# Linear attention and a low-rank mixer on one core: batch 0's q loaded, featured and transposed by halves of its heads

## The chip, the cores and the metric

The kernel runs on one core of one Trainium2 chip. The metric is the time of one execution on the device in microseconds, as the median of the timed runs; the profile is of one execution of its own.

## The reference

There are two parts, one behind the other, for 8 batches of 576 rows; attention has 8 heads of 64 columns, the mixer works on 512 columns.

```python
theta = pi / 2 * arange(S) / S
phi(x) = concat([relu(x) * cos(theta), relu(x) * sin(theta)])      # 64 -> 128 features
q_p, k_p = phi(q), phi(k)
kv  = einsum('bhsf,bhsd->bhfd', k_p, v)
z   = sum(k_p, axis=2)
x   = einsum('bhsf,bhfd->bhsd', q_p, kv) / (einsum('bhsf,bhf->bhs', q_p, z) + 1e-6)
x   = x with the heads side by side: (8, 576, 512)
u   = x + (x^T @ U @ V)^T                       # U: 576 x 32, V: 32 x 576
out = u + relu(u @ w_ch1) @ w_ch2               # 512 -> 2048 -> 512
```

Inputs and output are float32; the kernel multiplies in bf16.

## The kernel before

A batch's 576 rows are nine for each of 64 row groups, which are laid on 128 partitions: even partitions take five of the nine (chunks 0 to 3 and a tail, chunk 4), odd partitions take four. So a batch of q, k or v comes in two loads: `load_odd` (L80, 64 partitions x 8 heads x 256 columns, 512 KiB) and `load_even` (L74, 64 x 8 x 320, 640 KiB). Both take a range of heads; batch 0's v uses it and comes in four loads. SyncE issues them in program order: q, k and v of batch 0 first.

The schedule is written out by hand: each engine executes its instructions in the order of the program text, and an instruction that waits holds up what stands behind it on its engine. The program has a long list of slots from batch 0's first mixer matmuls on, in which TensorE is fed without a stop, and a part ahead of it, which the change touches. That part, for batch 0, goes like this:

- `keep_warm` issues matmuls of a zero tile (L202), four of 512 and 72 of 128 columns, while the first loads are on their way.
- `q_prep` (by `prep` and `scaled_relu`, L305 on ScalarE, L307 on VectorE) makes the features of one chunk of q: relu times the cosine weight on VectorE, relu times the sine weight on ScalarE, each 128 x 512. For chunk 3 VectorE makes both (`FEATS`). `qtr_mm` (L394) transposes a chunk's eight heads on TensorE into a bank `t_q[c]`, and one 512-wide filler follows each chunk.
- `qtr_evac` (by `cast`, L114 on ScalarE, L116 on VectorE) copies a bank into `q_pT` or, for the tail, `q_tlT`. Chunks 0 to 2 are copied ahead of k's features, chunk 3 and the tail behind them, both on ScalarE.
- `k_prep` makes k's features in the order 0, 1, 2, 4, 3, and `z_mm` (L1219) sums each chunk with 48 columns of ones, eight matmuls a chunk, into a tile `xz`. `spread_v` (L235) spreads the small matrix V over four quarters.
- `first_chain` casts v to bf16 (`v0`), copies z, and interleaves on TensorE: `kv0_mm` (L353) for heads 0 and 1, `den_mm` (L1227) for chunks 0 to 2, `kv0_mm` for heads 2 and 3, `den_mm` for chunks 3 and 4. Then come the reciprocal (L429, L430), the products of q^T with kv (L1235), their division (L1244), kv of heads 4 to 7 (`kv_unit`, L341), and the mixer's first steps, up to `g1_open` (L727), which starts the dense part.

Weights come on GpSimd's queue. `mark` copies hold them back: `w1_load(0)` goes out once a one-element copy has read the tail of q's features, `w1_load(1)` to `(3)` once one has read `q_tlT`, and `w2_all` (L1385, in slot 6) once batch 1's `q_pT` is there; then four loads of w2 follow, a quarter (four of sixteen row blocks) each. SyncE's queue is held in the same way: q of batch 1 waits for k's first feature, k and v of batch 1 for z.

The functions that the change touches:

Of the kernel before, what the change touches and what calls it, by code (L numbers as in the profile page):

```python
# [17 lines left out]
def kernel(  # L18
# [11 lines left out]
    nc = tc.nc  # L30

    B = 8
    H = 8
# [3 lines left out]
    P = 128  # L37
# [11 lines left out]
    def tail(b):  # L49
# [23 lines left out]
    def load_even(dst, src, b, h0=0, h1=H):  # L73
        nc.sync.dma_start(  # L74
            out=dst[0:P:2, h0:h1].rearrange("m h c d -> m h (c d)"),
            in_=nines(src, b)[:, h0:h1, 0 : 5 * D],
        )
# [25 lines left out]
            out=w1_bf[:, :, cs], in_=moe_w_ch1.rearrange("(d p) n -> p d n", p=P)[:, :, cs]  # L103
        )

    def w2_load(n):
        js = slice(n * 4, n * 4 + 4)
        nc.gpsimd.dma_start(
            out=w2_bf[:, js, :], in_=moe_w_ch2.rearrange("(j p) n -> p j n", p=P)[:, js, :]
        )  # L110

    def cast(eng, o, i):
        if eng is nc.scalar:
            nc.scalar.activation(out=o, in_=i, func=AF.Copy, bias=0.0, scale=1.0)  # L114
        else:
            eng.tensor_copy(out=o, in_=i)  # L116


    V_, A_, G_ = nc.vector, nc.scalar, nc.gpsimd
# [4 lines left out]
    zero = pool.tile([P, 512], BF16, tag="o_sb", bufs=2, name="zero")  # L124
# [1 line left out]
    for x in (qst, kst, vst):  # L126
        V_.memset(x[:, :, 4, :], 0.0)
    load_odd(qst, q, 0)
    load_even(qst, q, 0)
    load_odd(kst, k, 0)  # L130
    load_even(kst, k, 0)
    for h0 in (0, 4):
# [2 lines left out]
    v0 = pool.tile([P, H, 5, D], BF16, tag="hid", bufs=1, name="v0")  # L135

    def load_uv():
# [16 lines left out]
        out=iota[:, 0:4], pattern=[[2, 4]], base=0, channel_multiplier=9,  # L154
        allow_small_or_imprecise_dtypes=True,
    )
    for lo in (0, TS):
        nc.gpsimd.iota(
            out=iota[lo : lo + TS, 4:5], pattern=[[1, 1]], base=8, channel_multiplier=18,
# [3 lines left out]
        out=iota[:, 5:6], pattern=[[1, 1]], base=8, channel_multiplier=9,  # L163
# [21 lines left out]
    q_tl = const.tile([P, H, 2 * D], BF16)  # L185
    q_tlT = const.tile([P, H, P], BF16)
    x_tl = const.tile([P, DM], BF16)
    U_bf = const.tile([P, 6, R], BF16)
    V_bf = const.tile([P, 4, P], BF16)
# [9 lines left out]
    def keep_warm(n, tag, bufs, cols=512):  # L199
        w_ps = ps.tile([P, 512], FP32, tag=tag, bufs=bufs, name="w_ps")  # L200
        for _ in range(n):
            nc.tensor.matmul(  # L202
                out=w_ps[:, 0:cols], lhsT=zero[:, 0:P], rhs=zero[:, 0:cols], start=True, stop=True
            )
# [3 lines left out]
    mark = const.tile([TS, 1], FP32)  # L208
# [141 lines left out]
    def kv0_mm(b, acc, hs):  # L350
        for h in hs:
            for c in range(5):
                nc.tensor.matmul(  # L353
                    out=acc[:, h, :], lhsT=k_p[b][:, c, h, :] if c < 4 else k_tl[:, h, :],
                    rhs=v0[:, h, c, :], start=(c == 0), stop=(c == 4),
                )
# [35 lines left out]
    def qtr_mm(b, c, h0, h1, t):  # L392
        for h in range(h0, h1):
            nc.tensor.transpose(  # L394
                out=t[:, h, :], in_=q_p[b][:, c, h, :] if c < 4 else q_tl[:, h, :],
                identity=ident,
            )

    def qtr_evac(b, c, eng, t):
        if c < 4:  # L400
            cast(eng, q_pT[b][:, c, :, :], t)
        else:
            cast(eng, q_tlT[:, :, tail(b)], t[:, :, 0:P:2])
# [634 lines left out]
    ORD = (4, 0, 1, 2, 3)  # L1038
# [185 lines left out]
    def den_mm(b, d, cs):  # L1224
        for c in cs:
            for h in range(H):
                nc.tensor.matmul(  # L1227
                    out=d[:, c, h, :], lhsT=qT_of(b, c, h),
                    rhs=z_sb[:, h : h + 1].to_broadcast([P, 12]), start=True, stop=True,
                )  # L1230
# [39 lines left out]
                scale=rec[rows, c, h0 + i : h0 + i + 1],  # L1270
            )

    def first_chain(b, xz, z, v_ps):
        def fill(n):
            for _ in range(n):
                nc.tensor.matmul(
                    out=xz[:, 1, P:512], lhsT=zero[:, 0:P], rhs=zero[:, 0:384],
                    start=True, stop=True,
                )

        d = xz[:, 1, 0:480].rearrange("p (c h n) -> p c h n", h=H, n=12)
        rec = pool.tile([P, 5, H], FP32, tag="rec5", bufs=1, name="rec5")
        cast(V_, v0[:, 0:2], vst[:, 0:2])
        cast(V_, z_sb, z[:, :, 0])
        cast(V_, v0[:, 2:4], vst[:, 2:4])
        cast(V_, v0[:, 4:6], vst[:, 4:6])
        qtr_evac(b, 4, A_, t_q[4])
        kv_sb[b] = pool.tile([P, H, E], BF16, tag="kv", bufs=2, name="kv")
        acc = bank([P, 4, D], FP32, *G3, "kv_ps")
        kv0_mm(b, acc, (0, 1))  # L1290
        den_mm(b, d, (0, 1, 2))
        kv0_mm(b, acc, (2, 3))
        cast(A_, V_bf, v_ps.rearrange("r (c p) -> r c p", c=4))
        cast(A_, kv_sb[b][:, 0:4, 0:D], acc)
        cast(A_, v0[:, 6:H], vst[:, 6:H])
        den_mm(b, d, (3, 4))
        recip(rec, d[:, :, :, 0])
        x0 = [xh_mm(b, c, 0, *G3) for c in ORD[0:2]]
        kv_unit(b, 1, *T1, A_)
        x0 += [xh_mm(b, c, 0, *t) for c, t in zip(ORD[2:5], (G3, OA, OB))]  # L1300
        xh_norm_act(b, ORD[4], 0, rec, x0[4])
        for n in range(4):
            xh_norm(b, ORD[n], 0, rec, x0[n])
# [24 lines left out]
        open_mm(b, 3, uT_ps[b, 3], range(4))  # L1328
# [2 lines left out]
    qT_alloc(0)  # L1331
    cast_uv()
    keep_warm(4, "X", 1)
    keep_warm(72, "X", 1, P)
    t_q = []
    for c in TL:
        tg = G3 if c < 3 else O2()
        t_q.append(bank([P, H, P], BF16, *tg, "t_ps"))
    for c in TL:
        q_prep(0, c, FEATS[c])  # L1340
        qtr_mm(0, c, 0, H, t_q[c])
        keep_warm(1, "X", 1)
    for c, eng in zip(TL[0:3], (V_, A_, V_)):
        qtr_evac(0, c, eng, t_q[c])
    xz = ps.tile([P, 2, 512], FP32, tag="X", bufs=1, name="xz")
    z = xz[:, 0, 0:384].rearrange("p (h n) -> p h n", n=48)
    v_ps = None
    for n, c in enumerate(KORD):
        k_prep(0, c, (V_, A_ if c < 4 else V_))
        if n < 2:  # L1350
            keep_warm((1, 2)[n], *T1)
        if n == 2:
            v_ps = spread_v(*T1)
        z_mm(0, c, z)
    qtr_evac(0, 3, A_, t_q[3])

    G_.tensor_copy(out=mark[0:1], in_=q_tl[0:1, 0, 0:1])
    w1_load(0)
    nc.sync.dma_start(out=mark2, in_=k_p[0][0:1, 0, 0, 0:1])
    load_odd(qst, q, 1)  # L1360
    load_even(qst, q, 1)
    first_chain(0, xz, z, v_ps)
    G_.tensor_copy(out=mark[0:1], in_=q_tlT[0:1, 0, 0:1])
    for n in range(1, 4):
        w1_load(n)
    nc.sync.dma_start(out=mark2, in_=z_sb[0:1, 0:1])
# [16 lines left out]

    def w2_all():
        G_.tensor_copy(out=mark[0:1], in_=q_pT[1][0:1, 3, 0, 0:1])  # L1385
        for n in range(4):
            w2_load(n)

    at(6, w2_all)
# [109 lines left out]
```

## Time and profile before

| | |
|---|---|
| time, median of 3 runs | 291.11 us (290.12 to 291.51) |
| the profiled execution, its own time | 290.06 us |
| its span | 288.3 us |
| TensorE, matmuls | 282.3 us busy, 98% |
| TensorE, weight loads | 211.8 us, 73% |
| VectorE | 218.6 us, 76% |
| ScalarE | 179.7 us, 62% |
| GpSimd | 71.3 us, 25% |
| moved by DMA | 53.32 MB, 185 GB/s over the span |

The profile of one execution names engines PE (TensorE matmuls), PEld (its weight loads), DVE (VectorE), ACT (ScalarE), POOL (GpSimd) and SP (SyncE); a q behind the name (SPq) stands for the engine's issuing side. A row of the timeline gives the start in us from the span's start, the length in us from the first start to the last end of the merged instructions, engine, line and operation, tile written and tiles read, shapes, and how many were merged; brackets hold idle time ahead of it and what ended it. Instructions overlap by a little, so an engine's pace is read from start to start. A row of the groups has the count, then the busy sum in us and the mean in ns. A row of the windows has the stretch, its length, the busy time with the count of instructions that touch it, the granted clock, the share of the DMA engines and GB/s. A row of the chain gives start, length and what the end waited for.

### The profile page before, as it was taken

What the parts mean: (1) busy time and instruction counts of PE and PEld (TensorE: products, weight loads), DVE (VectorE), ACT (ScalarE), POOL (GpSimd) and SP (SyncE); (2) the same over time, 40 slices, a digit from 0 to 9 for tenths busy, and PEclk for the clock granted to TensorE, in tenths of its full rate; (3) what the DMA queues carried; (4) which work ended last, traced back from release to release, by engine and by line L of the source; (5) the groups of instructions that cost most, each with busy time, mean ns of one, the idle gap of its engine ahead of it and who ended that gap; (6) DMA issues with size and microseconds to landing.
All of it is one profiled execution on the core that took longest, in us unless ns stands there. A gap on an engine that the chain in (4) does not pass through costs nothing.

```text
span 288.3 us, 7567 instructions
## 1 busy us (share of the span) xinstructions
PE 282.3 (98%) x3097; PEld 211.8 (73%) x3122; DVE 218.6 (76%) x449; ACT 179.7 (62%) x316; POOL 71.3 (25%) x111
## 2 busy tenths in 40 slices
PE   8999999999999999999999999999999999999995
PEld 6886455545887756876887667876888778899884
DVE  4979738886887688569895388958894689689864
ACT  2965651576687576986587588876797772177110
POOL 8330600050035304641006500351005000400140
PEclk9999999999999999999999999999999999999999
DMA  6999999999969999799829993489939400610023
GB/s 202 336 282 253 292 207 264 275 184 200 285 174 169 241 354 202 193 268 282 230 41 188 303 279 106 84 146 200 312 40 177 164 1 10 154 77 2 0 90 131
DMA packets 85447, 53.32 MB, mean 185 GB/s; under 512 B 53990, under 2 KB 83078, under 8 KB 85414
## 3 DMA queue, kind: packets, MB, share of 16 engines
q1 hardware_dynamic: 78998, 41.62, 61.5%
q0 software_dynamic: 6272, 11.17, 16.5%
q8 instruction: 24, 0.39, 0.5%
q10 hardware_dynamic: 144, 0.07, 0.1%
q14 instruction: 9, 0.07, 0.1%
HBM read 36.86 MB, written 9.44 MB: 161 GB/s over the span
## 4 chain that ended last, share of the span: by engine, by line
PE 97%; DVE 1%; issue 1%; DVEq 0%
PE w_ps L892 30%; PE g_ps L710 22%; PE al_ps L653 8%; PE be_ps L653 6%; PE gt_ps L741 5%; PE o_ps L781 5%; PE w_ps L202 3%; PE x_ps L439 3%; PE kv_ps L364 3%; PE ot_ps L801 2%; PE ot_ps L994 2%; PE a_ps L465 1%; PE va_ps L495 1%; PE t_ps L382 1%; PE t_ps L394 1%
## 5 line engine op out<-in xcount | busy, mean ns | idle before, releaser
L710 PE MATMUL g_ps<-uT,w_bf 128*128 128x512 bf16 x281 | 71.5, 380 | 0.7
L717 ACT ACTIVATE hid<-g_ps 128x512 bf16<-128x512 f32 x76 | 45.0, 597 | 26.2 <-PE g_ps L710 24.0
L912 POOL TENSOR_TENSOR o_sb<-o_sb,u_bf 128x512 f32<-128x512 f32 x21 | 25.6, 1232 | 110.6 <-DVE o_sb L912 110.6
L892 PEld LDWEIGHTS <-hid 128*128 128x128 bf16 x448 | 43.1, 98 | 5.7 <-DVE hid L857 0.2
L710 PEld LDWEIGHTS <-w_bf 128*128 128x128 bf16 x298 | 27.5, 98 | 23.8
L678 DVE TENSOR_TENSOR hid<-pw,be_ps 128x512 bf16<-128x512 f32 x39 | 26.7, 686 | 16.6 <-PE be_ps L653 9.4
L892 PEld LDWEIGHTS <-S 128*128 128x128 bf16 x336 | 32.2, 98 | 4.5
L114 ACT ACTIVATE pw<-al_ps 128x512 f32<-128x512 f32 x39 | 23.1, 595 | 15.4 <-PE al_ps L653 9.7
L892 PE MATMUL w_ps<-T,hid 128*128 128x256 bf16 x224 | 27.9, 273 | 0.0
L892 PE MATMUL w_ps<-w_bf,hid 128*128 128x256 bf16 x224 | 27.6, 273 | 0.0
L892 PE MATMUL w_ps<-T,S 128*128 128x256 bf16 x224 | 27.1, 273 | 0.0
L114 ACT ACTIVATE o_sb<-w_ps 128x512 f32<-128x512 f32 x21 | 12.5, 597 | 20.5 <-PE w_ps L892 14.1
L912 DVE TENSOR_TENSOR o_sb<-o_sb,w_ps 128x512 f32<-128x512 f32 x21 | 14.4, 685 | 13.7 <-ACT o_sb L114 9.6
L653 PEld LDWEIGHTS <-sa 128*128 128x128 bf16 x208 | 19.3, 98 | 4.9 <-issue 0.3
L506 DVE TENSOR_TENSOR u_bf<-x_bf,va_ps 128x1024 bf16<-128x1024 bf16 (+1 forms) x20 | 19.5, 1000 | 3.0 <-PE va_ps L495 3.0
L449 DVE TENSOR_TENSOR x_bf<-x_ps,rec 128x512 bf16<-128x512 f32 x28 | 19.4, 692 | 1.0
L116 POOL CAST v_ext<-vst 128x512 bf16<-128x512 f32 x24 | 16.4, 722 | 7.8 <-DMA vst<-in_v_dram 4.5
L653 PEld LDWEIGHTS <-w_bf 128*128 128x128 bf16 x156 | 15.2, 98 | 4.0 <-issue 0.2
L305 ACT ACTIVATE k_p<-kst,sinw 128x512 bf16<-128x512 f32 x26 | 18.0, 713 | 0.0
L741 PE MATMUL gt_ps<-uT_tl,w_bf 128*128 128x128 bf16 x256 | 16.4, 219 | 0.0
L653 PE MATMUL al_ps<-tb,sa 128*128 128x256 bf16 x104 | 15.6, 273 | 0.2
L781 PE MATMUL o_ps<-w_bf,hid 128*128 128x512 bf16 x61 | 15.3, 380 | 0.2
(192 smaller groups left out, 509.1 us busy)
## 6 DMA issues: line engine op xcount, KB each, us to landing
qst<-in_q_dram SPq DMA_DIRECT2D x14, 512.0 KB, 5.9
kst<-in_k_dram SPq DMA_DIRECT2D x14, 512.0 KB, 8.6
vst<-in_v_dram SPq DMA_DIRECT2D x12, 512.0 KB, 8.7
out_dram<-o_sb POOLq DMA_DIRECT2D x12, 512.0 KB, 6.7
w_bf<-in_moe_w_ch_dram POOLq DMA_DIRECT2D x8, 512.0 KB, 10.4
out_dram<-o_sb SPq DMA_DIRECT2D x4, 512.0 KB, 3.0
qst<-in_q_dram SPq DMA_DIRECT2D x2, 640.0 KB, 5.7
kst<-in_k_dram SPq DMA_DIRECT2D x2, 640.0 KB, 13.8
```

The lines of the kernel that those rows point to most:

```text
L114: nc.scalar.activation(out=o, in_=i, func=AF.Copy, bias=0.0, scale=1.0)
L305: nc.scalar.activation(out=o, in_=i, func=AF.Relu, bias=0.0, scale=w)
L449: nc.vector.tensor_tensor(out=x_of(b, c, rows).rearrange("p (g i d) -> p g i d", g=2, d=D), in0=view[:, :, :, 0:D], in1=rec[rows].unsqueez ...
L506: nc.vector.tensor_tensor(out=u_bf[b][:, d0 : d0 + n], in0=x_bf[b].rearrange("p c (d n) -> p d c n", n=P)[:, d0 : d0 + n], in1=t.rearrange ...
L653: nc.tensor.matmul(out=res[:, k_, :], lhsT=lhs[:, d, k_, :], rhs=rhs[:, d, :], start=(opens and k_ == 0 and d == 0), stop=(k_ == 1 and d = ...
L678: V_.tensor_tensor(out=o, in0=x, in1=res, op=ALU.add)
L710: nc.tensor.matmul(out=g_ps.rearrange("p (c t) -> p c t", c=4), lhsT=w1_bf[:, d, j * P : j * P + P], rhs=uT[b][:, d, :, :], start=(d == 0) ...
L717: nc.scalar.activation(out=hid[b][:, j, :], in_=g_ps, func=AF.Relu, bias=0.0, scale=1.0)
L741: nc.tensor.matmul(out=g_ps[:, jj, :], lhsT=w1_bf[:, d, j * P : j * P + P], rhs=uT_tl[pr][:, d, :], start=(d == 0), stop=(d == 3),)
L781: nc.tensor.matmul(out=o, lhsT=hid[0][:, j, cc * P : cc * P + P], rhs=w2_bf[:, j, :], start=(j == 0), stop=(j == NJ - 1),)
L892: nc.tensor.matmul(out=res[:, g, :], lhsT=lhs[:, k_, g * P : g * P + P], rhs=rhs[:, k_, :], start=(opens and k_ == 0 and g == 0), stop=(k_ ...
L912: eng.tensor_tensor(out=o_, in0=x, in1=y, op=ALU.add)
```

## The change

1. Batch 0's even rows of q come in two loads, heads 0 to 3 and heads 4 to 7, behind the odd rows, which stay one load.
2. The narrow fillers at the start are 28 in place of 72. q's features and transposes go through the five chunks for heads 0 to 3, then for heads 4 to 7, so each feature is 128 x 256; four narrow fillers follow each of the first three chunks, and the 512-wide ones go.
3. `spread_v` stands behind the transposes. All five chunks of q^T are copied ahead of k's features: 0, 2 and 3 on VectorE, 1 and the tail on ScalarE. 32 narrow fillers follow on TensorE.
4. k's features are shared out by `FEATS` too: VectorE makes both of chunk 3, ScalarE the sine of the others (the tail's included). One filler of 384 columns stands between the groups of `z_mm`. V's cast stands ahead of `first_chain`.
5. In `first_chain` v's casts are four on VectorE, two of them ahead of z's copy and none on ScalarE; the matmuls of kv of heads 0 to 3 come in one piece ahead of all denominators, which start with the tail.
6. The gates: `w1_load(0)` waits for the copy of chunk 2 of q^T, the other three for z's copy. w2's first quarter comes in two loads of two row blocks.

```diff
-    def w2_load(n):
-        js = slice(n * 4, n * 4 + 4)
+    def w2_load(n, i=0, w=4):
+        js = slice(n * 4 + i, n * 4 + i + w)
...
     load_odd(qst, q, 0)
-    load_even(qst, q, 0)
+    load_even(qst, q, 0, 0, 4)
+    load_even(qst, q, 0, 4, H)
...
-        cast(V_, v0[:, 0:2], vst[:, 0:2])
+        for h in (0, 2):
+            cast(V_, v0[:, h : h + 2], vst[:, h : h + 2])
         cast(V_, z_sb, z[:, :, 0])
-        cast(V_, v0[:, 2:4], vst[:, 2:4])
-        cast(V_, v0[:, 4:6], vst[:, 4:6])
-        qtr_evac(b, 4, A_, t_q[4])
+        for h in (4, 6):
+            cast(V_, v0[:, h : h + 2], vst[:, h : h + 2])
...
-        kv0_mm(b, acc, (0, 1))
-        den_mm(b, d, (0, 1, 2))
-        kv0_mm(b, acc, (2, 3))
-        cast(A_, V_bf, v_ps.rearrange("r (c p) -> r c p", c=4))
+        kv0_mm(b, acc, range(4))
         cast(A_, kv_sb[b][:, 0:4, 0:D], acc)
-        cast(A_, v0[:, 6:H], vst[:, 6:H])
-        den_mm(b, d, (3, 4))
+        den_mm(b, d, ORD)
...
-    keep_warm(72, "X", 1, P)
+    keep_warm(28, "X", 1, P)
...
-    for c in TL:
-        q_prep(0, c, FEATS[c])
-        qtr_mm(0, c, 0, H, t_q[c])
-        keep_warm(1, "X", 1)
-    for c, eng in zip(TL[0:3], (V_, A_, V_)):
+    for h0 in (0, 4):
+        for c in TL:
+            q_prep(0, c, FEATS[c], h0, h0 + 4)
+            qtr_mm(0, c, h0, h0 + 4, t_q[c])
+            if h0 == 0 and c < 3:
+                keep_warm(4, "X", 1, P)
+    v_ps = spread_v(*T1)
+    for c, eng in ((0, V_), (1, A_), (2, V_), (4, A_), (3, V_)):
         qtr_evac(0, c, eng, t_q[c])
+    keep_warm(32, "X", 1, P)
...
-    for n, c in enumerate(KORD):
-        k_prep(0, c, (V_, A_ if c < 4 else V_))
-        if n < 2:
-            keep_warm((1, 2)[n], *T1)
-        if n == 2:
-            v_ps = spread_v(*T1)
+    for c in KORD:
+        k_prep(0, c, FEATS[c])
         z_mm(0, c, z)
-    qtr_evac(0, 3, A_, t_q[3])
+        if c != KORD[-1]:
+            fill(xz, 1)
+    cast(A_, V_bf, v_ps.rearrange("r (c p) -> r c p", c=4))
 
-    G_.tensor_copy(out=mark[0:1], in_=q_tl[0:1, 0, 0:1])
+    G_.tensor_copy(out=mark[0:1], in_=q_pT[0][0:1, 2, 0, 0:1])
     w1_load(0)
...
-    G_.tensor_copy(out=mark[0:1], in_=q_tlT[0:1, 0, 0:1])
+    G_.tensor_copy(out=mark[0:1], in_=z_sb[0:1, 0:1])
     for n in range(1, 4):
         w1_load(n)
...
-        for n in range(4):
+        for i in (0, 2):
+            w2_load(0, i, 2)
+        for n in range(1, 4):
             w2_load(n)
```

`fill`, which was unused inside `first_chain`, now stands outside it and issues 384-wide matmuls of the zero tile into the free half of `xz`.

More of the change, by code (lines that the diff above doesn't have):

```diff
@@ L1271, in xh_norm_act, with fill, first_chain @@
             )
[L1273 to L1279, printed above, removed]
+    def fill(xz, n):
+        for _ in range(n):
+            nc.tensor.matmul(
+                out=xz[:, 1, P:512], lhsT=zero[:, 0:P], rhs=zero[:, 0:384],
+                start=True, stop=True,
+            )
+    def first_chain(b, xz, z):
         d = xz[:, 1, 0:480].rearrange("p (c h n) -> p c h n", h=H, n=12)
         rec = pool.tile([P, 5, H], FP32, tag="rec5", bufs=1, name="rec5")
-        cast(V_, v0[:, 0:2], vst[:, 0:2])
+        for h in (0, 2):
+            cast(V_, v0[:, h : h + 2], vst[:, h : h + 2])
         cast(V_, z_sb, z[:, :, 0])
-        cast(V_, v0[:, 2:4], vst[:, 2:4])
-        cast(V_, v0[:, 4:6], vst[:, 4:6])
-        qtr_evac(b, 4, A_, t_q[4])
+        for h in (4, 6):
+            cast(V_, v0[:, h : h + 2], vst[:, h : h + 2])
         kv_sb[b] = pool.tile([P, H, E], BF16, tag="kv", bufs=2, name="kv")
         acc = bank([P, 4, D], FP32, *G3, "kv_ps")
-        kv0_mm(b, acc, (0, 1))
-        den_mm(b, d, (0, 1, 2))
-        kv0_mm(b, acc, (2, 3))
-        cast(A_, V_bf, v_ps.rearrange("r (c p) -> r c p", c=4))
+        kv0_mm(b, acc, range(4))
         cast(A_, kv_sb[b][:, 0:4, 0:D], acc)
-        cast(A_, v0[:, 6:H], vst[:, 6:H])
-        den_mm(b, d, (3, 4))
+        den_mm(b, d, ORD)
         recip(rec, d[:, :, :, 0])
@@ L1338 @@
         t_q.append(bank([P, H, P], BF16, *tg, "t_ps"))
-    for c in TL:
-        q_prep(0, c, FEATS[c])
-        qtr_mm(0, c, 0, H, t_q[c])
-        keep_warm(1, "X", 1)
-    for c, eng in zip(TL[0:3], (V_, A_, V_)):
+    for h0 in (0, 4):
[6 more added lines that the diff above has]
+    for c, eng in ((0, V_), (1, A_), (2, V_), (4, A_), (3, V_)):
         qtr_evac(0, c, eng, t_q[c])
+    keep_warm(32, "X", 1, P)
     xz = ps.tile([P, 2, 512], FP32, tag="X", bufs=1, name="xz")
     z = xz[:, 0, 0:384].rearrange("p (h n) -> p h n", n=48)
-    v_ps = None
-    for n, c in enumerate(KORD):
-        k_prep(0, c, (V_, A_ if c < 4 else V_))
-        if n < 2:
-            keep_warm((1, 2)[n], *T1)
-        if n == 2:
-            v_ps = spread_v(*T1)
+    for c in KORD:
+        k_prep(0, c, FEATS[c])
         z_mm(0, c, z)
-    qtr_evac(0, 3, A_, t_q[3])
-    G_.tensor_copy(out=mark[0:1], in_=q_tl[0:1, 0, 0:1])
+        if c != KORD[-1]:
+            fill(xz, 1)
+    cast(A_, V_bf, v_ps.rearrange("r (c p) -> r c p", c=4))
+    G_.tensor_copy(out=mark[0:1], in_=q_pT[0][0:1, 2, 0, 0:1])
     w1_load(0)
@@ L1361 @@
     load_even(qst, q, 1)
-    first_chain(0, xz, z, v_ps)
-    G_.tensor_copy(out=mark[0:1], in_=q_tlT[0:1, 0, 0:1])
+    first_chain(0, xz, z)
+    G_.tensor_copy(out=mark[0:1], in_=z_sb[0:1, 0:1])
     for n in range(1, 4):
```

## The prediction

> **What bounds the kernel now.** I read the page's busy times first, then the windows, then the timeline of the first 22 us engine by engine, then the chain of waits for the same stretch.
>
> ```profile
> span 288.3 us, 7567 instructions
> ...
> PE 282.3 (98%) x3097; PEld 211.8 (73%) x3122; DVE 218.6 (76%) x449; ACT 179.7 (62%) x316; POOL 71.3 (25%) x111
> ```
>
> ```profile
> 21.30:38.50 17.20, 17.04 (x121) 1.00 1.17 262
> ```
>
> TensorE is busy for 98% of the span, and from 21.3 us on for 17.04 of 17.20 us. So nothing that happens beside it after 21.3 us shortens the kernel; what counts is when that dense part can begin. Part of the 98% is filler (matmuls of a zero tile, w_ps L202), so ahead of 21.3 us a busy TensorE proves nothing. There the timeline has to be read:
>
> ```profile
> 7.53 1.95 ACT L305 ACTIVATE q_p<-qst,sinw 128x512 bf16<-128x512 f32 x3 [2.52 <-DMA qst<-in_q_dram]
> 7.55 1.79 DVE L307 TENSOR_SCALAR q_p<-qst,cosw 128x512 bf16<-128x512 f32 x4 [3.18 <-DMA qst<-in_q_dram]
> 10.06 0.68 DVE L116 COPY q_pT<-t_ps 128x1024 bf16<-128x1024 bf16 x1
> 10.24 1.02 ACT L114 ACTIVATE q_pT<-t_ps 128x1024 bf16<-128x1024 bf16 x1
> 10.90 0.69 DVE L116 COPY q_pT<-t_ps 128x1024 bf16<-128x1024 bf16 x1 [0.17 <-PE t_ps L394]
> 11.16 2.55 ACT L305 ACTIVATE k_p<-kst,sinw 128x512 bf16<-128x512 f32 x4
> 11.51 1.27 DVE L307 TENSOR_SCALAR k_p<-kst,cosw 128x512 bf16<-128x512 f32 x3
> 13.48 0.48 DVE L307 TENSOR_SCALAR k_p<-kst,cosw 128x512 bf16<-128x512 f32 x1
> ...
> 14.51 0.59 ACT L114 ACTIVATE q_tlT<-t_ps 128x512 bf16<-128x512 bf16 x1
> ...
> 14.61 0.88 DVE L116 CAST v<-vst 128x640 bf16<-128x640 f32 x2
> 16.34 0.20 DVE L429 TENSOR_SCALAR rec<-xz 128x40 f32<-128x40 f32 x1 [0.84 <-PE xz L1227]
> ```
>
> Both engines wait for q until 7.53 and 7.55. After that VectorE is without a gap of note to the last feature of k (13.48 + 0.48 = 13.96). The chain of waits goes on from there:
>
> ```profile
> 13.79 0.70 PE xz L1219 x24
> 14.49 0.38 PE kv_ps L353 x10
> 14.87 0.62 PE xz L1227 x24
> 15.49 0.31 PE kv_ps L353 x10
> 15.80 0.51 PE xz L1227 x16
> ```
>
> The last z matmuls follow k's last feature and end at 14.49, 0.53 behind it. Then come 20 kv matmuls (0.38 + 0.31) and 40 denominator matmuls (0.62 + 0.51), 1.82 together, and 14.49 + 1.82 = 16.31 releases the reciprocal's first step at 16.34. So the path is q's landing, VectorE's queue, z, kv, denominators. A microsecond there is a microsecond of the end, for what follows is TensorE's own work.
>
> **The change part by part.**
>
> *When q's features can begin.* The even rows come in two loads, and heads 0 to 3 wait only for the odd load and the first of them.
>
> ```profile
> 3.00:5.96 2.96, 1.00 1.01 337
> DMA to landing us min/median/max: 5.7/5.7/5.7
> DMA to landing us min/median/max: 8.0/8.0/8.0
> DMA to landing us min/median/max: 8.4/8.4/8.5
> ```
>
> The first landing row is q's even load, issued at 1.70 (landed 7.4). The DMA engines move 337 GB/s, and the second half of that load is 320 KiB, 0.97 us at this rate. If the transfers stay in order, the first half lands that much sooner, and the features begin at 7.55 - 0.97 = 6.6. The ends: 6.0, if the odd rows are long in by then, and 7.5, if the loads share the engines and land together. I take 6.6, because batch 0's v already comes in such halves: the other two rows are its first load (issued at 3.76, landed 11.8) and its last two (issued at 5.10 and 5.87, landed 13.5 and 14.4). They land one after the other, 896 KiB in 2.6 us, 353 GB/s: the order is kept, and an extra load shows no fixed cost. [...] One more load also moves SyncE's queue: k's and v's loads are issued some 0.65 us later each, behind q bytes that are still moving, which hides it.
>
> *VectorE's queue, start to k's last feature.* Now: 13.96 - 7.55 = 6.41. Afterwards there are 12 half features, three copies of q^T in place of two (chunk 3 comes over from ScalarE), and six features of k as before (chunk 3's sine comes in, the tail's goes out). A whole k feature takes (13.48 - 11.51) / 5 = 0.394. No 128x256 feature is in the trace; the nearest rows are casts:
>
> ```profile
> L116 DVE CAST v_ext<-vst 128x1024 bf16<-128x1024 f32 x2 | 1.4, 694 | 0.0
> L116 DVE CAST v_tl<-vst 128x256 bf16<-128x256 f32 x2 | 0.6, 296 | 0.0
> ```
>
> 398 ns for 768 elements is 0.133 us for 256, so a half costs 0.394 - 0.133 = 0.26; the ends are 0.20 (half of a whole) and 0.30 (the 256 cast's full 296 ns). A copy takes 11.51 - 10.90 = 0.61 in the queue. The sum: 12 x 0.26 + 3 x 0.61 + 5 x 0.394 + 0.48 = 3.12 + 1.83 + 1.97 + 0.48 = 7.40, so k's last feature ends at 6.6 + 7.4 = 14.0, against 13.96: **+0.04**. The early start of 0.95 is eaten by the halves (0.6 more than six whole ones, which took 10.06 - 7.55 = 2.51) and the third copy (0.61), less the small waits between the two copies now.
>
> *ScalarE.* Eight half features, two copies, four k features.
>
> ```profile
> L717 ACT ACTIVATE hid<-g_ps 128x512 bf16<-128x512 f32 x18 | 10.4, 599 | 5.5 <-PE g_ps L710 5.5
> L114 ACT ACTIVATE kv<-kv_ps 128x256 bf16<-128x256 f32 x2 | 0.8, 386 | 0.8 <-PE kv_ps L341 0.5 <-PE kv_ps L353 0.2
> ```
>
> Half the columns save 0.213. A whole feature takes (2.55 - 0.71) / 3 = 0.61, so a half 0.40. The copies take 11.16 - 10.24 = 0.92 and at most 0.59. 6.6 + 3.2 + 0.92 + 0.59 + 2.55 = 13.86, which is 0.15 ahead of VectorE: no cost, unless a half takes over 0.42. V_bf's cast behind it is read by the matmuls of uT only near 19.6.
>
> *k's arrival.* k is used at 11.16 on ScalarE now, from about 11.2 afterwards, so it need not land sooner. The copies ahead of it use time in which k may still be on its way.
>
> *TensorE up to z.* The filler shrinks from 72 to 28 narrow matmuls, 12 go between the first chunks, 32 behind the transposes and four of 384 columns between the z groups. In the rows below eight transposes take 0.45, 0.056 each. The last transposes end near 10.2, spread_v's 0.3 and 32 x 0.056 = 1.8 lead to 12.3; the first k feature is ready at 6.6 + 3.12 + 1.83 + 0.48 = 12.0. So z starts 0.3 late and catches up by the last group: z's end near 14.5, as now. The ends are 0 and +0.3; I take +0.05.
>
> *Behind z.* All 20 kv matmuls now stand ahead of all 40 denominators: the same 1.82. The z cast waits behind two v casts (14.0 + 0.88, so it is done near 15.0); its readers come at 14.55 + 0.69 = 15.24. Cover 0.2; beyond it the price is one for one. v's last two heads go to VectorE, which has 0.84 idle ahead of L429. They are cast by 15.9, and kv_unit's matmuls want them near 16.6.
>
> *Gates on the weights.* w1's first load follows the copy of chunk 2 (11.0, now 10.2).
>
> ```profile
> 10.32 0.81 POOL L102 DMA_DIRECT2D w_bf<-in_moe_w_ch_dram  x1
> DMA to landing us min/median/max: 7.3/7.3/7.3
> 30.20 2.97 POOL L108 DMA_DIRECT2D w_bf<-in_moe_w_ch_dram  x4 [0.28 <-issue]
> DMA to landing us min/median/max: 7.7/7.7/7.7
> 38.46 1.03 PE L781 MATMUL o_ps<-w_bf,hid 128*128 128x512 bf16 x4
> ```
>
> It landed at 10.32 + 7.3 = 17.6 and is read at 21.3: 0.9 later is hidden. w2's first quarter landed at 30.20 + 7.7 = 37.9 and is read at 38.46, a cover of 0.56. In two parts, the second is issued 2.97 / 4 = 0.74 later but holds the same last bytes; it is read by the third matmul, 0.4 later. Between 0 and 0.2 us; I take 0. POOL's V_qt casts and later quarters move by 0.74, and the quarters have microseconds of cover.
>
> **The sum:** 0.04 + 0.05, about +0.1 us. The profiled execution took 290.06 (1.76 beside its span), so 290.2 in its terms. It is 1.05 below the median of the three timed runs, so I forecast 291.11 + 0.1 = **291.2**.
>
> **The rivals.** *First, slower: TensorE runs the transposes at half rate.*
>
> ```profile
> 1.19 1.90 PE w_ps L202 x4
> 3.13 5.96 PE w_ps L202 x72
> 9.09 0.45 PE t_ps L394 x8
> 21.37 0.97 PE g_ps L727 x4
> 5.00:7.00 2.00, 2.00 (x22) 1.00 1.08 340
> 7.00:7.50 0.50, 0.50 (x13) 1.00 1.07 322
> ```
>
> Four 512-wide matmuls took 1.90 at first and 0.97 later, and the count goes from 22 in two microseconds to 13 in half of one at 7 us, while the granted-clock column shows 1.00 throughout. With 0.112 and 0.056 for a narrow one, 72 in 5.96 put the switch at 7.0, after 5.8 us of unbroken matmuls. Now the filler would end by 3.13 + 28 x 0.112 = 6.3, and TensorE waits for the first half's features until about 7.1. If the switch needs the unbroken run, the first half's transposes and fillers (32 matmuls by chunk 4's end) take 32 x 0.112 = 3.6 from 7.1, to 10.7. Chunk 0's second half is then done at 10.9 where VectorE would copy it at 9.7: +1.2. If the rate stays low through the second half, copies follow transposes at 0.45 a chunk, +1.7. So 292.3 to 292.8. It decides if the switch has not come by 6.3. For it: this trace switched later. Against it: the timed runs may switch sooner, and most of a busy stretch may do. The Trainium skill, "TensorE: Matmul & The Clock Gate", Part 1, states that a free-running window of about 3.4 us of activity lifts a halved clock; the rows agree in rate and order of time, and by that page the moment varies from run to run, so a median could fall on either side. Chance 0.25.
>
> *Second, faster: the first half lands at 6.0 and a half feature costs 0.25.* Then 6.0 + 7.3 = 13.3, -0.65, so 290.5. For it: v's orderly landings. Against it: TensorE's 32 fillers alone reach 12.3, so z can hardly end 0.65 sooner. Chance 0.15.
>
> *Third, the split does nothing: both halves land at 7.5.* VectorE's queue then ends at 14.9, +0.95, 292.1. v's landings speak against it. Chance 0.10.
>
> **How the numbers follow.** My forecast has 0.50: VectorE's halves and landing within their inner bounds, 290.8 to 291.7. The range reaches from 290.0 (the second rival, with half a microsecond for the median's own scatter) to 292.8 (the first rival's upper price). About 0.5%, 1.46 us, is what a measurement of this kernel can tell from no change. No term of the sum gives 1.46 less; 0.08 for faster stands for the microsecond between this profile and the median, which the trace cannot show. Slower by over 1.46 needs the first rival's upper price, or its lower with one of the costs above, or the third with a dear half feature: 0.24. Within: 0.68.
>
> **What would show it.** Right: q's first half feature starts near 6.6 on both engines, a VectorE half takes 0.26 in the queue, k's last feature ends near 14.0, and L429's counterpart starts within 0.3 of 16.34. Wrong: a first copy of q^T after 10.5 behind transposes at over 0.1 us each (first rival), k's last feature before 13.5 (second), features that begin after 7.3 (third), or an idle TensorE at the first o_ps matmul near 38.5.

## The result, and the profile after

| | median of the timed runs | runs | profiled execution | its span |
|---|---|---|---|---|
| before, beside it | 290.45 us (289.79 to 291.51) | 9 | 290.06 us | 288.3 us |
| changed | 292.17 us (291.10 to 292.35) | 9 | 292.17 us | 290.4 us |

The ratio is 1.0049 [1.0033, 1.0065], which is 1.4 us (1.0 to 1.9) on 290.45. The medians themselves are 1.7 apart. The time lies inside the forecast range (290.0 to 292.8), and the ratio, at 0.49%, on the very edge of the 0.5% that the prediction took for no change; the likeliest case was +0.1, so 1.3 us and more have to be explained.

First what did not change. This is the window view of the changed kernel (columns: window, TensorE's busy time and count, granted clock, DMA share, GB/s), its last row from the first g_ps matmul at 23.34 on, which began at 21.30 before:

```profile
8.00:8.50 0.50, 0.50 (x11) 0.94 1.10 374
8.50:9.00 0.50, 0.50 (x8) 0.50 1.06 361
9.00:11.00 2.00, 2.00 (x22) 0.50 1.08 362
...
11.50:12.00 0.50, 0.50 (x9) 0.64 1.08 361
12.00:12.50 0.50, 0.50 (x11) 1.00 1.09 355
23.34:40.60 17.26, 17.10 (x121) 1.00 1.17 260
```

The dense part is as dense as before. From its start to the end of the span are 290.4 - 23.34 = 267.06 us, before 288.3 - 21.30 = 267.0. So the two profiles differ ahead of the dense part alone, by 2.04. The timeline there, TensorE's rows first, then GpSimd's and VectorE's:

```profile
1.19 4.55 PE L203 MATMUL w_ps<-zero 128*128 128x512 bf16 x32 [1.19 <-DVE zero L125]
7.89 0.38 PE L395 MATMUL t_ps<-ident,q_p 128*128 128x128 bf16 x4 [2.15 <-POOL v_four L116]
...
10.78 1.58 PE L395 MATMUL t_ps<-ident,q_p 128*128 128x128 bf16 x16
...
6.39 1.49 POOL L116 CAST v_four<-st_uv 32x256 bf16<-32x256 f32 x3
...
13.05 0.81 POOL L102 DMA_DIRECT2D w_bf<-in_moe_w_ch_dram  x1
...
6.95 0.79 DVE L308 TENSOR_SCALAR q_p<-qst,cosw 128x256 bf16<-128x256 f32 x1 [2.58 <-DMA qst<-in_q_dram]
6.95 1.72 DVE L308 TENSOR_SCALAR q_p<-qst,cosw 128x256 bf16<-128x256 f32 x4 [2.58 <-DMA qst<-in_q_dram]
...
9.12 1.13 DVE L308 TENSOR_SCALAR q_p<-qst,cosw 128x256 bf16<-128x256 f32 x4
10.16 0.34 DVE L308 TENSOR_SCALAR q_p<-qst,sinw 128x256 bf16<-128x256 f32 x1
10.43 0.34 DVE L308 TENSOR_SCALAR q_tl<-qst,cosw 128x256 bf16<-128x256 f32 x1
11.46 2.01 DVE L116 COPY q_pT<-t_ps 128x1024 bf16<-128x1024 bf16 x3 [0.69 <-PE t_ps L395]
13.38 0.70 DVE L308 TENSOR_SCALAR k_p<-kst,cosw 128x512 bf16<-128x512 f32 x1
...
15.58 0.47 DVE L308 TENSOR_SCALAR k_p<-kst,sinw 128x512 bf16<-128x512 f32 x1
...
18.38 0.20 DVE L430 TENSOR_SCALAR rec<-xz 128x40 f32<-128x40 f32 x1 [0.65 <-PE xz L1228]
```

(The first two VectorE rows are the first half feature by itself and the first four together.) Along VectorE's queue, term by term: the features begin at 6.95 where 6.6 was forecast (+0.35). The first six halves take 9.12 - 6.95 = 2.17 where 6 x 0.26 = 1.56 was forecast (+0.61), and the very first one 0.79. The second six take 1.57 (to 10.43 + 0.26 = 10.69), as forecast. The copies begin 0.77 after that, waiting for the transposes. They take 13.38 - 11.46 = 1.92 (+0.09), and k's six features 15.58 + 0.47 - 13.38 = 2.67 for 2.45 (+0.22), the first of them 0.70. Together +2.05: k's last feature ends at 16.05, not 14.0. From there to the reciprocal's first step are 2.33 us, forecast 2.35.

Why the copies wait is in the granted clock. TensorE stands idle from 5.74 to 7.89, takes up work at full clock, and at about 8.4 the clock falls to half for some 3.4 us. The idle row names GpSimd's cast of V as releaser; the transposes do not read that: what they wait for is the half feature, which ended at 6.95 + 0.79 = 7.74.

So there were three suspects: the half clock behind the idle stretch, GpSimd's work beside VectorE, and the split load itself.

### The profile page after: what moved, and what is told of

It reads as the page before. It is cut to its first block, busy times and chain, and to the rows that moved or that the text cites. A ratio compares the mean times of both kernels' runs of the same rounds, so it can differ in the third digit from the quotient of the medians.

```text
span 290.4 us, 7573 instructions
## 1 busy us (share of the span) xinstructions
PE 282.2 (97%) x3094; PEld 211.9 (73%) x3118; DVE 220.8 (76%) x457; ACT 179.0 (62%) x318; POOL 73.0 (25%) x112
## 4 chain that ended last, share of the span: by engine, by line
PE 95%; POOL 2%; issue 1%; DVE 1%; POOLq 0%; DVEq 0%
PE w_ps L893 30%; PE g_ps L711 22%; PE al_ps L654 8%; PE be_ps L654 6%; PE gt_ps L742 5%; PE o_ps L782 5%; PE x_ps L440 3%; PE kv_ps L365 2%; PE ot_ps L802 2%; PE ot_ps L995 2%; PE t_ps L395 1%; PE a_ps L466 1%; PE va_ps L496 1%; PE w_ps L203 1%; PE t_ps L383 1%
## 5 line engine op out<-in xcount | busy, mean ns | idle before, releaser
L116 POOL CAST v_ext<-vst 128x512 bf16<-128x512 f32 x24 | 17.0, 748 | 7.6 <-DMA vst<-in_v_dram 4.2
L306 ACT ACTIVATE k_p<-kst,sinw 128x512 bf16<-128x512 f32 x25 | 17.3, 714 | 0.0
```

Of the source, the lines that this page charges most:

```text
L306: nc.scalar.activation(out=o, in_=i, func=AF.Relu, bias=0.0, scale=w)
```

## The experiments

Times are medians, and ratios are to the kernel before, run beside each group (its medians were 290.3 to 290.5).

**1. More narrow fillers, so that TensorE isn't idle.**

```diff
-    keep_warm(28, "X", 1, P)
+    keep_warm(60, "X", 1, P)
```

> The changed kernel with 60 narrow fillers at the start in place of 28, so that TensorE has no gap between the fillers (which ended at 5.74 us in its profile) and the first transposes (7.89). Theory G (the gap halves TensorE's rate, and the copies of q^T wait for slow transposes): transposes at 0.056 us each throughout, granted clock 1.00 after the switch, the first copy of q^T near 10.8 instead of 11.46, the dense part (L728) near 22.7 instead of 23.34, 0.6 us less than the changed kernel. Theory Q (VectorE's queue of half features and copies sets the path): same as the changed kernel within 0.2 us, though the transposes are fast.

293.75 us (293.35 to 295.91), ratio 1.0115 [1.0086, 1.0145]: slower still. Its profile is of the slowest of its six runs (295.91 us; the others took 293.35 to 294.2, with a mean granted clock of 0.998 to 1.0):

```profile
10.48 1.87 DVE L116 COPY q_pT<-t_ps 128x1024 bf16<-128x1024 bf16 x3
17.27 0.20 DVE L430 TENSOR_SCALAR rec<-xz 128x40 f32<-128x40 f32 x1 [0.65 <-PE xz L1228]
23.37 0.27 PE L1259 MATMUL uT_ps<-ident,x_bf 128*128 128x128 bf16 x2 [1.72 <-issue]
24.27 1.03 PE L728 MATMUL g_ps<-uT,w_bf 128*128 128x512 bf16 x2
```

```profile
22.00:23.40 1.40, 0.03 (x1) 1.00 1.20 217
24.00:25.00 1.00, 1.00 (x4) 0.50 1.16 247
```

The first half worked as expected: the copies do not wait, and the reciprocal is 1.11 sooner than in the changed kernel. Then TensorE stops for 1.72 us between two matmuls of one loop, for nothing that the profile shows ("issue"), and the clock halves behind that stop as well. In this execution, what the fillers gave was lost there. What the other five runs lost is not in a profile; their clocks show no half clock.

**2. GpSimd kept away from q's features.** V is cast on ScalarE as it lands, U on ScalarE behind V_bf.

```diff
-                G_,
+                A_,
...
-        cast(G_, U_bf[:, 0:4, :], stU[:, 0:4, :])
+    def cast_u():
+        cast(A_, U_bf[:, 0:4, :], stU[:, 0:4, :])
```

> The changed kernel with the casts of V moved from GpSimd to ScalarE ahead of q's features, and those of U to ScalarE behind V_bf, so that GpSimd does nothing beside q's half features. Theory Q, contention part (VectorE's first half features took 0.79 and 0.44 us beside GpSimd's casts, later ones 0.34): all half features 0.34 long and 0.26 apart, VectorE through with q's features 0.6 us sooner (10.1 instead of 10.7). Alone it gives the end little, if transposes at half rate still hold the copies (theory G): then the first copy of q^T stays after 11.2 and the time within 0.3 us of the changed kernel. If theory G is wrong it gives 0.6 us.

291.84 us (290.45 to 293.12), ratio 1.0037 [1.0019, 1.0056]. In the profile (290.91 us, the third lowest of 12) the clock did not fall, and up to the reciprocal every step of VectorE's queue lies within 0.2 us of where the prediction's sum had put it:

```profile
6.47 1.14 DVE L310 TENSOR_SCALAR q_p<-qst,cosw 128x256 bf16<-128x256 f32 x4 [2.10 <-DMA qst<-in_q_dram]
9.66 1.90 DVE L116 COPY q_pT<-t_ps 128x1024 bf16<-128x1024 bf16 x3
13.67 0.47 DVE L310 TENSOR_SCALAR k_p<-kst,sinw 128x512 bf16<-128x512 f32 x1
16.48 0.20 DVE L432 TENSOR_SCALAR rec<-xz 128x40 f32<-128x40 f32 x1 [0.66 <-PE xz L1230]
...
39.39 0.59 PE L784 MATMUL o_ps<-w_bf,hid 128*128 128x512 bf16 x2 [0.20 <-DMA w_bf<-in_moe_w_ch_dram]
```

Halves 0.26 apart, k's last feature ending at 14.14, the reciprocal at 16.48, 0.14 behind the kernel before. The dense part begins 0.14 late too, at 21.44, but from there to the end are 267.7 us, 0.7 more than before. About half of that is the last row: the third o_ps matmul comes 0.36 late, because it waits for the second of w2's two loads, which landed at 39.35. The median does not follow this execution: half of the runs are over 291.8.

**3. Both together** (60 narrow fillers, V and U on ScalarE).

> Both edits of the two kernels before: 60 fillers, and V's and U's casts on ScalarE. If gap and contention together make up the loss: first copy of q^T near 10.1, dense part near 22.0, 1.3 us less than the changed kernel, which leaves 0.3 to 0.6 us over the kernel before (the half features' own cost and the third copy, less the earlier start). If something else makes the loss (the order of kv and denominators, the later weights): within 0.4 us of the changed kernel.

293.00 us (292.22 to 296.22), ratio 1.0105 [1.0065, 1.0144]. Again TensorE stops for "issue", for 0.95 us, ahead of the same matmul as in experiment 1 (at 22.80). V landed late as well, so that its casts held up ScalarE's features of q. Three of the eight runs have a fallen clock (0.993 or 0.994) and took 295.36 to 296.22. Missed.

**4. The split alone**, on the kernel before.

```diff
-    load_even(qst, q, 0)
+    load_even(qst, q, 0, 0, 4)
+    load_even(qst, q, 0, 4, H)
```

> The kernel before with batch 0's even rows of q in two loads and nothing else: features are still whole and wait for both. In the changed kernel the second half landed at 8.8 us, where the one load landed at 7.4. If the split itself delays the last bytes: q's features start near 8.9 instead of 7.55, and the kernel is 1.2 us slower than before. If the split costs nothing and the 8.8 came from k's loads going out beside it in another order: features start near 7.6 and the time is that of before within 0.3 us.

291.43 us (289.99 to 293.8), ratio 1.0027 [1.0002, 1.0052]. In its profile whole features begin at 7.86 (7.55 before), but the dense part starts at 21.23, no later than before. The four lowest of the 12 runs (289.99 to 290.49) are as fast as the kernel before beside it, whose median is 290.44; the other eight go from 290.91 to 293.8, and one of them has a fallen clock (0.993). So the split alone, with nothing that makes use of it, is slower by a little, barely clear of the noise. What takes that time isn't in the one profile, which is of the fourth lowest run (290.49).

**5. Wider fillers, the same number of instructions.**

```diff
-    keep_warm(28, "X", 1, P)
+    keep_warm(20, "X", 1, 180)
+    keep_warm(8, "X", 1)
```

> The changed kernel with its 28 narrow fillers made wider (20 of 180 columns, 8 of 512), so that TensorE is busy from 1.2 to about 7.6 us while the number of its instructions stays what it was. If the cost is the idle TensorE between the fillers' end (5.74) and the first half feature: no half clock between 8.4 and 11.9, transposes at 0.06 each, the first copy of q^T near 10.5 without a wait, the reciprocal's first step near 17.3 instead of 18.38, the dense part near 22.3 instead of 23.34, and the time 1.0 us (0.7 to 1.2) below the changed kernel's; the slow first half features of VectorE stay. If the loss of 60 fillers came from the number of instructions ahead of uT's matmuls (a supply in blocks), there is no wait of 1 us without a releaser in uT here. If that wait comes from the fillers' time, or from the earlier start of the dense part, it is here too, and the time is 293 or more.

292.90 us (291.5 to 293.22), ratio 1.007 [1.0047, 1.0093]. TensorE is busy to the first transposes at 7.33, the clock stays at 1.00, and there is no stop for "issue". But the second half of q's even rows, issued at 2.4, landed at 10.5 in this execution:

```profile
6.40 1.58 POOL L116 CAST v_four<-st_uv 32x256 bf16<-32x256 f32 x3
...
6.52 1.88 DVE L308 TENSOR_SCALAR q_p<-qst,cosw 128x256 bf16<-128x256 f32 x4 [2.15 <-DMA qst<-in_q_dram]
10.50 1.14 DVE L308 TENSOR_SCALAR q_p<-qst,cosw 128x256 bf16<-128x256 f32 x4 [1.58 <-DMA qst<-in_q_dram]
18.88 0.20 DVE L430 TENSOR_SCALAR rec<-xz 128x40 f32<-128x40 f32 x1 [0.65 <-PE xz L1228]
```

The DMA engines moved 324 to 363 GB/s all the while, and it was not the order that had changed. A load's landing is counted in sixteen steps on its semaphore, and the trace has the time of each. Of the second half fifteen steps came by 7.49 us, as early as in experiment 2 (7.50), and the sixteenth at 10.48. For each load of k and v behind it on the queue it is the same: fifteen steps by the usual time, the last some 3 us later (of v's last load 13.96 and 16.84). Between 14 and 15 us, when all else has been moved, the engines' share is that of about one in sixteen (columns as in the window view above):

```profile
14.00:15.00 1.00, 0.94 (x18) 1.00 0.07 24
```

So the order was kept, as the forecast took it, but a sixteenth of the load came late. That this is the part of one DMA engine, and why it lagged, is not shown. The time missed the expectation.

**6. Wider fillers, and V cast on GpSimd as soon as it lands** (its memsets moved behind the weights' issues, U on ScalarE).

> The same wider fillers, and GpSimd kept away from VectorE's first half features: V is cast on GpSimd as soon as it lands (its memsets of later use come behind the weights' issues), U on ScalarE behind V_bf. If GpSimd's casts made VectorE's first halves slow (0.79 for the first, 2.17 for six instead of 1.56), the first takes under 0.5 here, the first copy of q^T starts near 10.0, the reciprocal's first step at 16.5 to 16.9, the dense part at 21.5 to 21.9, and the time is within 0.5 us of the kernel before. If the first halves were slow for another reason (the transfers still landing in the same rows), nothing is won on the wider fillers alone: 17.3 and 22.3.

291.32 us (290.53 to 293.06), ratio 1.0038 [1.0014, 1.0061]. The profile (290.53 us, the lowest of 12 runs) kept to the expectation up to the dense part:

```profile
5.88 1.50 POOL L116 CAST v_four<-st_uv 32x256 bf16<-32x256 f32 x3 [1.07 <-DMA st_uv<-in_moe_V_dram]
6.73 1.33 DVE L306 TENSOR_SCALAR q_p<-qst,cosw 128x256 bf16<-128x256 f32 x4 [2.36 <-DMA qst<-in_q_dram]
16.88 0.20 DVE L428 TENSOR_SCALAR rec<-xz 128x40 f32<-128x40 f32 x1 [0.65 <-PE xz L1226]
21.84 1.47 PE L726 MATMUL g_ps<-uT,w_bf 128*128 128x512 bf16 x6
```

VectorE's first four half features take 1.14 with no GpSimd beside them (experiment 2), 1.33 with its casts of V to 7.38 (here), 1.72 in the changed kernel with casts to 7.88, and 1.88 with casts to 7.98 (experiment 5). That is 0.65, 0.93 and 1.46 us of overlap: the longer, the dearer. The uT matmuls come sooner here than in experiments 1 and 3, and TensorE does not stop. Those two had 32 more fillers, so it is not the early start that brings the stop; the number of instructions ahead is what is left, from one profile of each.

**7. The changed kernel again**, one run.

> The changed kernel as it is, once more, to see whether the half clock of 8.4 to 11.9 comes in each execution or by chance. If an idle TensorE of 2 us brings it each time: granted clock near 0.5 for over 3 us somewhere between 8 and 12.5, and the reciprocal's first step at 18.0 to 18.5. If it is chance: full clock throughout, and the first step near 17.3.

293.13 us. No half clock this time, though TensorE idled 1.74 us:

```profile
7.33 1.28 DVE L308 TENSOR_SCALAR q_p<-qst,cosw 128x256 bf16<-128x256 f32 x4 [2.96 <-DMA qst<-in_q_dram]
7.90 0.38 PE L395 MATMUL t_ps<-ident,q_p 128*128 128x128 bf16 x4 [1.74 <-POOL v_four L116]
10.64 1.87 DVE L116 COPY q_pT<-t_ps 128x1024 bf16<-128x1024 bf16 x3
17.43 0.20 DVE L430 TENSOR_SCALAR rec<-xz 128x40 f32<-128x40 f32 x1 [0.65 <-PE xz L1228]
22.39 1.47 PE L728 MATMUL g_ps<-uT,w_bf 128*128 128x512 bf16 x6
200.73 0.43 PE L440 MATMUL x_ps<-kv,q_pT 128*128 128x65 bf16 x8 [1.89 <-DMA q_pT<-q_p]
```

At full clock the start is 1.09 late: the features begin at 7.33 (+0.73), the first six halves cost +0.17, k's features +0.21. The late start is again a late sixteenth: of the first half fifteen steps came by 6.33, the last at 7.21. A second loss is far from the change: at 200.7 TensorE waits 1.89 us for a transposing DMA of q^T (fifteen steps by 198.82, the last at 200.68). The profiles of before and of the changed kernel don't show such a wait, and those of experiments 1, 4 and 5 do (1.3, 0.2 and 0.3).

**8. w2's two loads alone**, on the kernel before.

> The kernel before with only w2's first quarter in two loads. If that part is free, as the prediction has it: the time within 0.3 us of the kernel before, the first o_ps matmul right behind the last g matmul near 38.5. If each software-issued load costs its issue or a fixed part on the path: the first o_ps matmuls wait, up to 0.8 us, and the time is that much longer.

290.32 us, ratio 0.9997 [0.9982, 1.0012]: free, as forecast.

**9. The changed kernel with the even rows in one load.**

> The changed kernel with q's even rows in one load again; features of four heads at a time, the three early copies, the fewer fillers and w2's two loads stay. By the prediction's sum the features then begin at 7.4 to 7.6, VectorE needs 7.4 to 7.6 to k's last feature, the reciprocal's first step comes at 17.2 to 17.5 at full clock and the dense part at 22.2 to 22.5: 0.9 to 1.2 us above the kernel before, and a further 1.0 where the clock falls, for TensorE now idles 2.4 us ahead of the features. If the split's second landing is what costs in most executions, this kernel is at the changed kernel's time or below it, with the scatter of the kernel before.

292.27 us (291.19 to 293.59), ratio 1.0045 [1.0024, 1.0067]. The five runs with a mean granted clock of 1.0 took 291.19 to 291.58, the five at 0.994 or below 292.17 to 293.59 (two at 0.998: 292.47 and 293.31). The profile is of a run at 0.992:

```profile
7.64 1.21 DVE L307 TENSOR_SCALAR q_p<-qst,cosw 128x256 bf16<-128x256 f32 x4 [3.26 <-DMA qst<-in_q_dram]
8.19 0.40 PE L394 MATMUL t_ps<-ident,q_p 128*128 128x128 bf16 x4 [1.98 <-POOL U_bf L116]
18.52 0.20 DVE L429 TENSOR_SCALAR rec<-xz 128x40 f32<-128x40 f32 x1 [0.60 <-PE xz L1227]
```

At full clock its runs lie 0.7 to 1.1 above before, which is the sum's 0.95 for features at 7.5. The half clock costs about one more. The median is that of the changed kernel (292.17), so in the median the split neither won nor lost anything there.

**10. The kernel before, with q asked for sooner** (qst's zeros first, the even rows on ScalarE's queue at 1.43 instead of 1.70, k's even rows ahead of its odd ones, 60 fillers).

> The kernel before with q's even rows asked for sooner and in one load: qst's zeros are written first, the load is issued on ScalarE's queue as soon as they are there (1.35 instead of 1.70), k's even rows ahead of its odd ones, and 60 narrow fillers for 72. If the time of issue sets q's landing: features at 7.1 to 7.3 (7.53 and 7.55 before), the reciprocal's first step at 15.9 to 16.1, and 0.2 to 0.4 us less than the kernel before. If the transfers share the engines, k's bytes come in beside q's, the features begin at 7.5 or later and nothing is won.

290.60 us, ratio 0.9994 [0.9976, 1.0013]: nothing won. The features begin at 7.51 all the same. V landed later, and GpSimd's casts fell on whole features: 2.37 for the four where they took 1.79.

```profile
7.26 1.85 POOL L116 CAST v_four<-st_uv 32x256 bf16<-32x256 f32 x3 [0.92 <-DMA st_uv<-in_moe_V_dram]
7.51 2.37 DVE L308 TENSOR_SCALAR q_p<-qst,cosw 128x512 bf16<-128x512 f32 x4 [3.14 <-DMA qst<-in_q_dram]
10.85 0.81 POOL L102 DMA_DIRECT2D w_bf<-in_moe_w_ch_dram  x1
11.78 0.47 DVE L308 TENSOR_SCALAR k_p<-kst,cosw 128x512 bf16<-128x512 f32 x1
```

**11. Experiment 6 with the even halves issued on ScalarE's queue** (and, as in experiment 10, qst's zeros first and k's even rows ahead of its odd ones).

> The kernel with the wider fillers and V cast as soon as it lands, and q's two even halves issued on ScalarE's queue at 1.35 and 2.0. If the time of issue sets the landing: first half features at 6.3 to 6.5 (6.71 and 6.73 without), the reciprocal's first step at 16.4 to 16.6, the dense part near 21.4, and 0.3 us less than without. If k's bytes come in beside the second half, that lands after 8.1 and the engines wait for it, up to 1 us, and the time is the same or longer.

291.55 us (290.80 to 292.76), ratio 1.0023 [1.0005, 1.0041]. The first half landed sooner (features at 6.31) and the second only at 8.8, and both engines then waited for k, 0.5 us and more: the reciprocal came at 17.73. A late sixteenth is in this too: k's two loads had fifteen steps by 10.00 and 11.50 and the last at 11.19 and 12.69, and k's features begin at 12.8, where the copies ahead of them were done at 12.1 on ScalarE and 12.3 on VectorE.

**12. Experiment 9 with wider fillers** (18 of 180 columns, 10 of 512 for the 28 narrow ones).

> The changed kernel with q's even rows in one load again, and its 28 narrow fillers made wider at the same count (18 of 180 columns, 10 of 512), so that TensorE has work to 7.8 us instead of 6.2. Without the wider fillers, 5 of 12 timed runs had a mean granted clock of 0.987 to 0.994 and took 292.2 to 293.6; those at 1.0 took 291.2 to 291.6. If the idle stretch ahead of the features is what lowers the clock: no run at 0.994 or below, the features at 7.5, the reciprocal's first step at 17.1 to 17.4, the dense part at 22.0 to 22.4, and a median of 291.2 to 291.6, 0.7 to 1.0 below the same kernel with narrow fillers. If the clock falls by chance, 2 or more of 12 runs are at 0.994 or below and the median is 291.9 or more.

292.20 us (291.23 to 294.00), ratio 1.0059 [1.0037, 1.0081]. One run of 12 was at 0.994 or below, for 5 of 12 with narrow fillers, which speaks for the idle stretch as what brings the half clock on. The median did not follow. In this profile q's even rows, in one load as before, landed at 8.84 (fifteen steps by 7.48):

```profile
8.97 1.14 DVE L307 TENSOR_SCALAR q_p<-qst,cosw 128x256 bf16<-128x256 f32 x4 [4.60 <-DMA qst<-in_q_dram]
13.59 0.81 POOL L102 DMA_DIRECT2D w_bf<-in_moe_w_ch_dram  x1
13.92 0.70 DVE L307 TENSOR_SCALAR k_p<-kst,cosw 128x512 bf16<-128x512 f32 x1
```

No kernel of these beats the kernel before.

## Why the prediction was right or wrong

*What bounds the kernel* held: all of the start's 2.04 us is found again in the span, and in the eight profiles in which TensorE never waits over 0.15 us behind it, the dense part takes 266.9 to 267.1 us to the end. *VectorE's own terms* held: a half feature is 0.26 in the queue (rows of experiment 2), a copy 0.60 to 0.64, and 2.33 us lead from k's last feature to the reciprocal. In the one execution where nothing disturbed the start (experiment 2) the sum of +0.1 came out as +0.14 there. w1's landing, V_bf and z's cast cost nothing, as said. w2's two loads cost nothing in the median (experiment 8), but their cover was put too high: the second load landed 9.0 and 8.8 us after the first one's issue in experiments 2 and 9, where the one load took 7.7 before and 8.5 in experiment 4, and the third o_ps matmul came 0.36 and 0.14 late.

That the time fell into the range is owed to the range's width and in part to luck. Its upper end was set for the first rival, whose reason did not come about. And the forecast of 291.2 stood on three runs of the kernel before with a median of 291.11; nine runs beside the changed kernel gave 290.45. So the change cost 1.7 us by the medians where +0.1 was summed up, while the time is only 1.0 above the forecast.

Four steps failed.

*"I take 6.6"* for the features' start. The profiles with the split, both halves asked for on SyncE's queue and halves computed, show 6.47, 6.52, 6.68, 6.73, 6.87, 6.95 and 7.33; the second half landed between 7.5 and 10.5. Unsplit the features began at 7.5 to 7.7 in four profiles and at 8.97 in one. The order was kept, as read from v's landings: fifteen of the first half's sixteen steps came by 6.2 to 6.7 in all seven. What the reading of one execution could not show is that the sixteenth may come late, by up to 0.9 us for the first half and 3.0 for the second. The third rival's sign, features after 7.3, came about once (experiment 7) by this, not by halves that land together. That "an extra load shows no fixed cost" is in doubt as well: the split alone raised the median by 1.0, with a ratio that only just leaves 1 out (experiment 4).

*GpSimd beside the halves* was not in the sum. They were costed as if VectorE were alone. GpSimd's casts of V (6.39 to 7.88) had lain almost wholly ahead of the features at 7.55; bringing the features forward put them beside the casts, for +0.61 in the profile and +0.17 in experiment 7. The row shown of before already had a hint: 1.79 for four features that are 0.394 apart in k's rows. The Trainium skill, "SBUF — State Buffer", section "SBUF: two separate sides", says that GpSimd and VectorE's instructions in a two-port mode share a pair of ports, an exclusive lock that is held for a whole instruction. The rows would fit that (0.79 for a half that takes 0.35 alone, experiment 2); that these features run in such a mode no run here shows.

*The moved gate.* w1's first load was priced by its landing alone. Its issue is 0.81 us of GpSimd, and behind chunk 2's copy it starts 0.33 ahead of VectorE's first k feature: 0.70 instead of 0.48. In all nine profiles in which the issue lies beside that feature, the first three take 1.47 to 1.49; in the five in which it is over first, 1.26 to 1.28 (before and experiments 4, 8, 10 and 11). That is the +0.2 of k's features. No run moved the gate alone.

*TensorE's rate*, the first rival. Its price (+1.2 to +1.7) and its sign in the trace (a first copy after 10.5 behind transposes of 0.1 us) came about in the profile; its reason was another. The switch to the full rate did not come late: the fillers were at it from about 5.2 on (4 wide ones in 1.9 us, then 28 narrow ones in 2.65, where 28 x 0.112 = 3.1 at half rate). The clock was taken back after 2.15 us of idling. Among the kernels with 28 narrow fillers, 10 of 34 timed runs had a mean granted clock of 0.994 or less, which is 3.4 us at half clock in 290 (0.5 x 3.4 / 290 = 0.006); of those with wide ones 1 of 42; of the kernel before none of the 94 runs beside experiments 1 to 12. So it is the price of some runs, not of the median: of the changed kernel's nine runs the six without it took 291.1 to 292.3. The Trainium skill, "TensorE: Matmul & The Clock Gate", Part 1, has the clock halved after an idle window of about 3.4 us and warns of gaps longer than that. Here gaps of 1.72, 1.98 and 2.15 us were enough, and ones of 1.74 and 1.58 were not; that the half clock lasted 3.4 us agrees with a window of that length.

What stays open is the median. The steps above give +0.1 to +1.1 at full clock and some 1.0 more in the runs with a fallen clock. But the kernels of experiments 2 and 6, in which GpSimd's part was taken away or lessened, in experiment 6 the idle stretch too, keep medians 1.4 and 0.9 above before, while the dense part begins only 0.1 and 0.5 late in their profiles, which are of fast runs. Seen in profiles are late sixteenths of q or k (experiments 5, 7, 11 and 12, and the second half of the changed kernel: fifteen steps by 7.94, the last at 8.79), waits for w2 (experiment 2) and the wait at 200 us (experiments 1 and 7). One was seen with the start as it was before, too: in experiment 8 v's last load had fifteen steps by 14.45 and the last at 15.84. So a late sixteenth does not need the split. How often each happens in the timed runs, and whether the split or wider fillers make it more frequent, is not shown.

## What to carry to other kernels

When work is brought forward, list what runs on every engine in the stretch that it moves into: a GpSimd cast or the issue of a GpSimd load that was harmless made one VectorE instruction take 0.79 instead of 0.35 here, another 0.70 instead of 0.48. Filler that keeps TensorE's clock up has to reach to the new start of its work; made wider, it came without the stop that more of it brought, but no median here got below that of the kernel before by it. A landing that one trace shows is one draw: it is as late as its latest part, and a term that rests on it deserves the widest range of the sum.

## What the runs showed of the hardware that was not expected

The stop for "issue" of 1.72 and 0.95 us, twice ahead of the same matmul in the kernels with 32 more matmuls in front than the changed kernel, and not at that place in the others. The profile names a DMA queue "instruction"; whose instructions it brings it does not say. Of the whole of experiment 1:

```profile
q8 instruction: 24, 0.39, 0.6%
```

24 packets of about 16 KB. One of them falls between 20.0 and 21.6 us, right ahead of the stop; in the kernel before one falls between 15 and 20 and none between 20 and 25. With the DMA engines at a share of 1.20 (the window row of experiment 1) instructions that arrive late would explain a stop at one place of the program, and why it moved in with 32 more matmuls. That is argued from two profiles and not shown.

The late sixteenth, too: one of a load's sixteen steps came up to 3.0 us behind the fifteenth while the others kept their time (experiment 5), and the loads behind it on the queue then had the same lag.
